# A gated mix of attention and a token MLP on one core: zeros, key sets, query transfers and value buffers scheduled anew

## The chip, the cores and the metric

The kernel runs on one core of a Trainium2 chip. The time is the device time of one execution in microseconds (us), the median of several runs. The core has these engines, each with its own instruction list that it works through in order: TensorE (PE; its weight loads are PEld), VectorE (DVE), ScalarE (ACT), GpSimd (POOL) and SyncE (SP, which here issues transfers and passes semaphores on). Transfers run on 16 DMA engines that the issuing engine's queue feeds.

## What is computed

The input x has 2048 tokens of 448 numbers. A gate weighs two branches, multi-head attention with 16 heads of 28 and a token-wise MLP of width 1792:

```python
x = A_x
g = _sigmoid((x * gate_w).sum(-1, keepdims=True))
a = _A_ref(x, A_wqkv, A_wo)      # softmax(q k^T * 28**-0.5) v, heads joined, @ wo
b = _B_ref(x, B_w1, B_b1, B_w2, B_b2)   # gelu(layernorm(x) @ w1 + b1) @ w2 + b2
return g * a + (1 - g) * b
```

All in fp32. Products on PE take fp32 in a rounded form (fp32r), so the kernel splits operands into a high part and a low part (value minus high) and sums three products; hence names like `hh`/`hl`, `ka`/`la`, `yh`/`yl`.

## The kernel before

**Three stages.** The first (0 to about 129 us) projects x to queries and keys (`QK`, stored to the DRAM tensor `qk`) and to values (`Val`, stored to `vs`). The second (to about 447 us) is the MLP in four chunks of 512 tokens: `Up` (x @ w1, one piece for each of 14 blocks of 128 of the width, then GELU on ACT) and `Down` (@ w2, one piece for each of four token tiles). The third is attention: scores, exponentials, products with the values, then the output projection.

**Four strips.** In the first two stages nearly every matmul contracts over 32 rows, a quarter of PE's array, and four of them run beside each other, one in each *strip* of 32 rows. A piece is done strip by strip; when a strip has finished its share, a semaphore passed through SP (`hand`, line 512) lets the next strip continue in the same PSUM bank. The class `Strips` plans all of this in Python while the kernel is built: it keeps a clock for each strip and engine from a table of costs, and lets each strip take the next matmul that its clock allows. Its result is a fixed instruction list for each engine. Tasks with a due time (`st.at(time, fn)`) are put into the lists when the planner's clock passes that time; `st.get(t, kb)` is its estimate of when a transfer of kb KB is in place: it queues all transfers noted so far at 230 KB per us and adds 2.2 us.

**Row maxima.** Softmax needs the maximum of each score row. The class `RowMax` computes plain scores (line 199, keys `kd` and queries `qd`, 28 rows of one strip) and DVE reduces them from PSUM (line 201). There are 16 sets (four groups of four heads, four chunks of queries) of 64 products, 1024 in all. Strip j holds head j of the group. After the 16th product of a set in a strip, the planner schedules three kinds of task: a query load two sets ahead (`load_q`, line 185), at the end of a group a load of the next group's keys (`load_k`, line 179), both on SP, and the closing of the set. These products are slipped between the pieces; what is left of them when attention begins is done there. `self.hot[j]` is the planner's time from which strip j may use its keys.

**Low parts.** The closing of an `Up` piece is: ACT writes GELU to `h` (line 342, two buffers), ACT writes the high part `hh[f]` (line 343), POOL writes the low part `hl[f]` (line 350). `Down` reads both.

**From the MLP to attention.** When the last `Up` piece of the last chunk is closed, `early` schedules the first group's attention operands: POOL sets the key low-part tile `la` to zero (line 829), loads queries (`fetch_qq`, line 802) and keys (`fetch_kk`, line 785) through its own queue, loads values from `vs` (`load_v`, line 797), and splits keys and queries into high and low parts (lines 790, 791, 806, 807).

**Attention.** The main loop works in turns. A turn does five or six score blocks (line 1121, three products each on one strip), two exponentials on ACT (line 1125; one over three blocks, one over two or three) and products with the values (line 1133):

```python
owed = rowmax.left()
size = min(left, 5 if owed and owed > 2 * ((left - 116) // 6) else 6)
```

While many row maxima are owed, a turn has five blocks and leaves room for three of them on the strips that its blocks do not use; with six blocks there is room for two. The last group's turns also hold output projections (`project`, lines 970 to 972).

**Values.** `Val.close` copies a value tile from PSUM to one of three buffers `vt` (line 311) and then issues its transfer to `vs` on ACT's queue (line 315). POOL writes the buffers' constant columns at the very start (lines 842 and 843).

Of the kernel before, what the change touches and what calls it, by code (L numbers as in the profile page):

```python
# [7 lines left out]
F32 = mybir.dt.float32  # L8
# [7 lines left out]
P = 128  # L16
S = 2048
D = 448
H = 16
# [16 lines left out]
def kernel(ctx: ExitStack, tc: tile.TileContext, xt, wqk, wv, wo, xk, w1, b1, w2, b2,  # L36
                          ident_d, sel_d, out):
    nc = tc.nc
# [35 lines left out]
    bk = banks.tile([P, 8, CH], F32, name="bk")  # L74
# [3 lines left out]
    px = p0.enter_context(tc.tile_pool(name="px", bufs=1))  # L78
# [42 lines left out]
    mr = px.tile([P, 2, NT], F32, name="mr")  # L121
    mrt = px.tile([P, 2 * NT], F32, name="mrt")
    std = px.tile([P, NT], F32, name="std")
    vt = [px.tile([P, H, 32], F32, name=f"vt{i}") for i in range(3)]

    bxr = [px.tile([P, 2, D], F32, name=f"bxr{i}") for i in range(2)]

# [96 lines left out]
    rowmax = RowMax()  # L224
# [63 lines left out]
    class Val(Piece):  # L288
# [18 lines left out]
            return ops  # L307

        def close(self, st, now):
            v, ps, tt = vt[self.i % 3], bk[:, self.bank], self.i  # L310
            nc.scalar.activation(v[:, :, 0:DH], ps[:, :D].rearrange("p (h d) -> p h d", d=DH), AF.Copy)
            nc.scalar.activation(zall[:, tt:tt + 1], ps[:, D:D + 1], AF.Copy)
            st.use("act", now + 0.2, 0.75)
            st.free[self.bank] = st.act + 0.1
            st.at(st.act + 0.3, lambda: nc.scalar.dma_start(vs[tt], v.rearrange("p (g j) d -> p g (j d)", g=NG)), act=0.35)
# [75 lines left out]
    class Strips:  # L391
# [92 lines left out]
        def rowmax(self, s, now):  # L484
            if now < self.hot[s] or not rowmax.ready(s):
                return False
            if rowmax.cnt[s] > 5 + min(rowmax.cnt):
                return False
            b = min(self.rm, key=lambda b: self.rm[b])
            if self.rm[b] > now:  # L490
                return False
            ends = rowmax.one(s, bk[:, b])
            self.t[s] = now + 0.232
            self.use("dve", now + 0.45, RM)
            self.rm[b] = self.dve + 0.1
            for kind, n, j in ends:
                if kind == "q":
                    self.at(now + 1.5, lambda n=n, j=j: rowmax.load_q(n, j))
                elif kind == "k":
                    self.at(now + 1.5, lambda n=n, j=j: rowmax.load_k(n, j))  # L500
                    self.hot[j] = now + 8.0
                else:
                    self.at(now + 0.5, lambda n=n: rowmax.close(n), dve=0.45)
                    self.at(now + 3.0, lambda n=n: rowmax.store(n))
            return True
# [277 lines left out]
    def fetch_kk(g, j):  # L783
        r = D + (4 * g + j) * DH
        loads[0].dma_start(klo[g][32 * j:32 * j + DH].bitcast(F32), qk[r:r + DH])

    def split_kk(g, i):
        sl = slice(i * CH, (i + 1) * CH)
        h, l = khi[g][:, sl], klo[g][:, sl]
        nc.gpsimd.tensor_copy(h, l.bitcast(F32))  # L790
        nc.gpsimd.tensor_sub(l, l.bitcast(F32), h.bitcast(F32))
# [27 lines left out]
    def early(st, now):  # L819
# [5 lines left out]
        ka, kb, la, lb = (ak.tile([P, S], F32R, name=n) for n in ("ka", "kb", "la", "lb"))  # L825
        va, vb = (ak.tile([P, NT, P], F32, name=n) for n in ("va", "vb"))
        for d, a, b in ((khi, ka, kb), (klo, la, lb), (vg, va, vb)):
            d.update({0: a, 1: b, 2: a, 3: b})
        st.at(now + 0.5, lambda: nc.gpsimd.memset(la.bitcast(F32), 0.0), pool=2.2)
        for j in range(4):  # L830
            st.at(now + 3.5 + 1.5 * j, lambda j=j: fetch_qq(0, j))
            st.at(now + 4.0 + 1.5 * j, lambda j=j: fetch_kk(0, j))
            st.at(now + 13.0 + 2.0 * j, lambda j=j: split_kk(0, j), pool=1.9)
        st.at(now + 12.0, lambda: split_qq(0), pool=1.9)
        st.at(now + 10.0, lambda: load_v(0, slice(0, 8)))
        st.at(now + 11.5, lambda: load_v(0, slice(8, 16)))
# [19 lines left out]
    load = [("wq", 0)] + [("x", 0, t) for t in range(4)] + [("wq", 3), ("wq", 4)]  # L856
# [365 lines left out]
```

## Time and profile before

| | |
|---|---|
| median of 3 runs | 1092.6 us (1090.66 to 1093.17) |
| the profiled execution, its own time | 1092.28 us |
| its span, first to last instruction | 1090.3 us |
| mean TensorE clock granted | 0.999 |
| matmuls on PE | 13314 |
| row maxima on DVE | 1024 |
| exponentials on ACT (line 1125) | 395 |
| first score matmul (line 1121) | 448.61 us |
| last exponential begins | 1066.93 us |

A profile row of the timeline reads: start in us, length in us, engine and line, operation, output <- inputs, shapes, count, and in brackets how long the engine had been idle and what ended that. A row of the waits reads: who waited, for whom, us in total, how many times, the longest. A row of windows reads: stretch, length, then for each engine its busy time with the number of its instructions, the granted clock, the busy share of the DMA engines and GB/s. A releaser is the one that came last by the profile; where that one had long been done, it was another.

### The profile page before, as it was taken

The page shows a single profiled execution, that of the slowest core. Times are in us where ns is not written, and L with a number is a line of the kernel's source. Part 1 is how long each engine was busy: PE and PEld are TensorE (multiplying, and loading weights), DVE is VectorE, ACT ScalarE, POOL GpSimd, SP SyncE. Part 2 cuts the span into 40 slices and gives each one's busy share as a digit, 9 for nine tenths or more (in the row PEclk, how much of TensorE's full clock was granted, in tenths as well). Part 3 has the DMA queues.
Part 4 walks back from the last instruction along what each step waited for, and adds up shares of the span by engine and source line. Part 5 has one row for each costly group of instructions (what it writes and reads, how often), then busy time and mean ns, then how long its engine had stood idle before and what let it go on. Part 6 is the DMA issues. An engine that isn't in the chain of part 4 may idle for free.

```text
span 1090.3 us, 30784 instructions
## 1 busy us (share of the span) xinstructions
PE 1075.4 (99%) x13314; PEld 728.4 (67%) x13314; DVE 740.5 (68%) x1186; ACT 636.0 (58%) x668; POOL 364.1 (33%) x372
## 2 busy tenths in 40 slices
PE   9999999999999999999999999999999999999997
PEld 6999999999999999644444444444444444454555
DVE  4279998999999998667766766567667766421102
ACT  5324472142141151577878878878877888858571
POOL 3456687345242057321100110310011215345430
PEclk9999999999999999999999999999999999999999
DMA  6695433104100105410000000500002101011111
GB/s 231 207 307 191 168 119 113 43 5 103 38 9 11 38 9 127 115 44 27 16 17 19 23 23 17 125 17 12 23 18 61 50 16 54 25 52 38 61 53 60
DMA packets 47463, 73.17 MB, mean 67 GB/s; under 512 B 13632, under 2 KB 28608, under 8 KB 46416
## 3 DMA queue, kind: packets, MB, share of 16 engines
q1 hardware_dynamic: 33888, 39.11, 12.2%
q0 software_dynamic: 4800, 16.89, 5.4%
q10 hardware_dynamic: 8640, 15.21, 3.8%
q8 instruction: 104, 1.70, 0.6%
q14 instruction: 31, 0.25, 0.1%
HBM read 51.75 MB, written 19.31 MB: 65 GB/s over the span
## 4 chain that ended last, share of the span: by engine, by line
PE 95%; DVE 2%; ACT 1%; DMA 0%; issue 0%; POOL 0%; SPq 0%; ACTq 0%; DVEq 0%; POOLq 0%
PE bk L475 33%; PE bk L1133 22%; PE bk L1121 19%; PE bk L199 15%; PE bk L970 1%; DVE mx L201 1%; PE bk L971 1%; PE bk L972 1%; PE bk L886 1%; ACT p L1125 1%; DMA first<-in_xt 0%; DVE ob L992 0%; POOL hl L350 0%; DVE acc L977 0%; ACT h L342 0%
## 5 line engine op out<-in xcount | busy, mean ns | idle before, releaser
L201 DVE TENSOR_REDUCE mx<-bk 128x1 f32<-128x512 f32 x1024 | 672.2, 688 | 197.7 <-PE bk L199 159.0
L1125 ACT ACTIVATE p<-bk 128x1536 f32<-128x1536 f32 (+1 forms) x395 | 483.1, 1275 | 135.7 <-PE bk L1121 134.9
L199 PE MATMUL bk<-kd,qd 28*128 28x512 f32 x1024 | 447.4, 438 | 3.1 <-DVE mx L201 1.9
L199 PEld LDWEIGHTS bk<-kd,qd 28*128 28x128 f32 x1024 | 186.1, 182 | 197.2 <-DVE mx L201 133.9
L475 PE MATMUL bk<-yh,w1f 32*128 32x512 f32 x1568 | 183.3, 392 | 0.4 <-ACT gb L385 0.4
L475 PE MATMUL bk<-yl,w1f 32*128 32x512 f32 x784 | 160.8, 391 | 0.0
L475 PEld LDWEIGHTS bk<-yh,w1f 32*128 32x128 f32 x1568 | 151.4, 183 | 2.2 <-ACT gb L385 1.6
L475 PE MATMUL bk<-w2h,hh 32*128 32x448 f32 x896 | 133.3, 366 | 1.3 <-ACT hh L343 1.3
L475 PE MATMUL bk<-w2l,hh 32*128 32x448 f32 x896 | 132.6, 363 | 0.0
L1133 PE MATMUL bk<-p,va 128*32 128x512 f32 x1024 | 131.2, 602 | 0.0
L1133 PE MATMUL bk<-p,vb 128*32 128x512 f32 (+1 forms) x1168 | 129.6, 548 | 0.0
L350 POOL TENSOR_TENSOR hl<-h,hh 128x512 fp32r<-128x512 f32 x56 | 73.7, 1325 | 132.4 <-ACT hh L343 67.1
L806 POOL CAST yh<-yl 128x512 fp32r<-128x512 f32 x16 | 9.8, 613 | 294.1 <-DMA yl<-qk 121.7
L1121 PE MATMUL bk<-yh,ka 29*128 29x512 f32 x512 | 106.9, 482 | 0.3 <-ACT h L385 0.3
L475 PEld LDWEIGHTS bk<-yl,w1f 32*128 32x128 f32 x784 | 103.7, 183 | 0.2
L475 PEld LDWEIGHTS bk<-w2h,hh 32*128 32x128 f32 x896 | 99.0, 183 | 1.9 <-ACT hh L343 1.7
L475 PEld LDWEIGHTS bk<-w2l,hh 32*128 32x128 f32 x896 | 100.0, 183 | 0.2
L1121 PE MATMUL bk<-yh,kb 29*128 29x512 f32 x512 | 99.1, 479 | 0.8 <-ACT p L1125 0.6
L1121 PE MATMUL bk<-yh,la 28*128 28x512 f32 x512 | 88.4, 392 | 0.0
L385 ACT ACTIVATE gb<-bk 128x448 f32<-128x448 f32 x14 | 7.6, 546 | 138.5 <-PE bk L475 100.2
L475 PE MATMUL bk<-w2h,hl 32*128 32x448 f32 x896 | 87.7, 362 | 0.0
L1121 PE MATMUL bk<-yl,ka 28*128 28x512 f32 x512 | 87.1, 410 | 0.0
(141 smaller groups left out, 1598.1 us busy)
## 6 DMA issues: line engine op xcount, KB each, us to landing
qk<-qo ACTq DMA_DIRECT2D x28, 256.0 KB
raw<-in_xt SPq DMA_DIRECT2D x17, 256.0 KB
vs<-vt ACTq DMA_DIRECT2D x16, 256.0 KB
rc<-rls SPq DMA_DIRECT2D x60, 64.0 KB
bxr<-in_xk POOLq DMA_DIRECT2D x8, 448.0 KB, 6.2
acc<-gbs SPq DMA_DIRECT2D x16, 224.0 KB
out_y<-acc SPq DMA_DIRECT2D x16, 224.0 KB
qd<-qk SPq DMA_DIRECT2D x60, 56.0 KB
```

The source lines that it names most:

```text
L199: nc.tensor.matmul(ps, self.qd[n % 2][r, i * P:(i + 1) * P], self.kd[r, k * 512:(k + 1) * 512], start=True, stop=True)
L201: nc.vector.reduce_max(self.mx[n % 2][:, j, i, k:k + 1], ps, axis=AX)
L350: nc.gpsimd.tensor_sub(hl[f], h, hh[f].bitcast(F32))
L475: mm = nc.tensor.matmul(bk[:, x.bank, :n], a, b, start=x.first, stop=(len(x.rem) == 1 and m == len(ops) - 1), skip_group_check=True)
L806: nc.gpsimd.tensor_copy(h, l.bitcast(F32))
L886: nc.tensor.matmul(bk[:, b], w, v, start=(i == 0), stop=(i == len(ops) - 1), skip_group_check=True)
L970: nc.tensor.matmul(po, h, woh[:, g], start=(g == 0), stop=False, skip_group_check=True)
L971: nc.tensor.matmul(po, h, wol[:, g], start=False, stop=False, skip_group_check=True)
L972: nc.tensor.matmul(po, l, woh[:, g], start=False, stop=(g == NG - 1), skip_group_check=True)
L1121: nc.tensor.matmul(bk[:, turn_bank(i)], w[r, ks], q[r], start=(p == 0), stop=(p == 2), skip_group_check=True)
L1125: nc.scalar.activation(t[:, :count], bk[:, b:b + count], AF.Exp, scale=SCALE)
L1133: nc.tensor.matmul(bk[32 * j:32 * j + 32, 7, sl], vg[n // NC][:, k, 32 * j:32 * j + 32], prob[4 * b + j][:, sl], start=(k == 0), stop=(k = ...
```

## The change

Four edits. In `early` the zeros for `la` get a later due time, the key loads, and with them the key splits, too. In `Strips.rowmax` the query load is due 6.0 instead of 1.5 after the strip's last product of a set; and a strip's new keys may be used from the planner's own estimate of their landing plus 1.0, taken at the moment when the load is issued (until then never), instead of a fixed 8.0 after the last product. The key loads are now also noted in the planner's transfer queue. The value buffers become five.

```diff
-    vt = [px.tile([P, H, 32], F32, name=f"vt{i}") for i in range(3)]
+    vt = [px.tile([P, H, 32], F32, name=f"vt{i}") for i in range(5)]
...
-            v, ps, tt = vt[self.i % 3], bk[:, self.bank], self.i
+            v, ps, tt = vt[self.i % 5], bk[:, self.bank], self.i
...
                 if kind == "q":
-                    self.at(now + 1.5, lambda n=n, j=j: rowmax.load_q(n, j))
+                    self.at(now + 6.0, lambda n=n, j=j: rowmax.load_q(n, j))
                 elif kind == "k":
-                    self.at(now + 1.5, lambda n=n, j=j: rowmax.load_k(n, j))
-                    self.hot[j] = now + 8.0
+                    def load(n=n, j=j):
+                        rowmax.load_k(n, j)
+                        self.hot[j] = self.get(self.clock + 0.6, 224) + 1.0
+
+                    self.at(now + 1.5, load)
+                    self.hot[j] = 1e9
...
-        st.at(now + 0.5, lambda: nc.gpsimd.memset(la.bitcast(F32), 0.0), pool=2.2)
+        st.at(now + 4.0, lambda: nc.gpsimd.memset(la.bitcast(F32), 0.0), pool=2.2)
         for j in range(4):
             st.at(now + 3.5 + 1.5 * j, lambda j=j: fetch_qq(0, j))
-            st.at(now + 4.0 + 1.5 * j, lambda j=j: fetch_kk(0, j))
-            st.at(now + 13.0 + 2.0 * j, lambda j=j: split_kk(0, j), pool=1.9)
+            st.at(now + 6.5 + 1.5 * j, lambda j=j: fetch_kk(0, j))
+            st.at(now + 14.5 + 2.0 * j, lambda j=j: split_kk(0, j), pool=1.9)
```

Four lines are added, so a line behind the change has a number higher by four in the changed kernel (829 becomes 833). Because the planner draws the order from these times, the lists of PE, SP and DVE differ from the first change of key sets on. Three places follow; the numbers behind tile names only tell buffers apart.

POOL at the end of the last `Up` pieces, where `la` is set to zero, before:

```order
L350 TENSOR_TENSOR hl_2820<-h,hh_2806 128x512
L350 TENSOR_TENSOR hl_2821<-h,hh_2807 128x512
L829 MEMSET la 128x2048
L350 TENSOR_TENSOR hl_2822<-h,hh_2808 128x512
L350 TENSOR_TENSOR hl_2823<-h,hh_2809 128x512
L350 TENSOR_TENSOR hl_2824<-h,hh_2810 128x512
L802 DMA yl<-qk 28x512
L785 DMA la<-qk 28x2048
```

and with the change:

```order
L350 TENSOR_TENSOR hl_2826<-h,hh_2812 128x512
L350 TENSOR_TENSOR hl_2828<-h,hh_2814 128x512
L350 TENSOR_TENSOR hl_2827<-h,hh_2813 128x512
L350 TENSOR_TENSOR hl_2829<-h,hh_2815 128x512
L350 TENSOR_TENSOR hl_2830<-h,hh_2816 128x512
L806 DMA yl<-qk 28x512
L833 MEMSET la 128x2048
L806 DMA yl<-qk 28x512
L789 DMA la<-qk 28x2048
```

The zeros stood ahead of three low parts and stand behind all of them now, and ahead of three of the four query loads.

SP at the first change of key sets (`kd` keys, `qd` queries, `ms` maxima of a closed set, `raw` the next chunk's x), before:

```order
L220 DMA ms_74<-mt_156 4x32x32
L185 DMA qd_151<-qk 28x512
L179 DMA kd<-qk 28x2048
L185 DMA qd_151<-qk 28x512
L179 DMA kd<-qk 28x2048
L185 DMA qd_151<-qk 28x512
L179 DMA kd<-qk 28x2048
L185 DMA qd_151<-qk 28x512
L179 DMA kd<-qk 28x2048
L552 DMA raw_132<-in_xt 128x512
```

and with the change:

```order
L220 DMA ms_74<-mt_158 4x32x32
L185 DMA qd_152<-qk 28x512
L179 DMA kd<-qk 28x2048 x2
L185 DMA qd_153<-qk 28x512
L179 DMA kd<-qk 28x2048 x2
L556 DMA raw_132<-in_xt 128x512
```

A query load stood ahead of each of the four key loads; one is left between them, and the other three follow behind the loads of x.

ACT where the turns of five blocks end (128x1536 is an exponential over three blocks, 128x1024 over two), before:

```order
L1125 ACTIVATE p_14640<-bk 128x1536
L1125 ACTIVATE p_14652<-bk 128x1024
L1125 ACTIVATE p_14671<-bk 128x1536
L1125 ACTIVATE p_14683<-bk 128x1024
L1125 ACTIVATE p_14711<-bk 128x1536
L1125 ACTIVATE p_14723<-bk 128x1024
L1125 ACTIVATE p_14744<-bk 128x1536
L1125 ACTIVATE p_14756<-bk 128x1024
```

and with the change:

```order
L1129 ACTIVATE p_14662<-bk 128x1536
L1129 ACTIVATE p_14675<-bk 128x1536
L1129 ACTIVATE p_14694<-bk 128x1536
L1129 ACTIVATE p_14706<-bk 128x1024
L1129 ACTIVATE p_14734<-bk 128x1536
L1129 ACTIVATE p_14747<-bk 128x1536
L1129 ACTIVATE p_14768<-bk 128x1536
L1129 ACTIVATE p_14780<-bk 128x1024
```

Turns of six appear earlier. In the whole list the exponentials over two blocks go from 161 to 158 and those over three from 234 to 236; the last turn has five blocks instead of three. The list of PE has 537 products of line 199 ahead of the first score matmul, where it had 529.

## The prediction

> **What bounds the kernel now.** I read the page first, then which waits TensorE (PE) ends on, then the places of those waits in time. The page:
>
> ```profile
> span 1090.3 us, 30784 instructions
> PE 1075.4 (99%) x13314; PEld 728.4 (67%) x13314; DVE 740.5 (68%) x1186; ACT 636.0 (58%) x668; POOL 364.1 (33%) x372
> ...
> L201 DVE TENSOR_REDUCE mx<-bk 128x1 f32<-128x512 f32 x1024 | 672.2, 688 | 197.7 <-PE bk L199 159.0
> ```
>
> PE is busy for 99% of the span, so the other engines matter only where they make it stop or make its list longer. What stops it from the key-set change to the scores, by the waits of PE between 240 and 450 us:
>
> ```profile
> engine line waited for: us in total, times, longest us
> PE bk L475 <- ACT hh L343: 1.3, 1, 1.3
> PE bk L199 <- DVE mx L201: 1.0, 1, 1.0
> PE bk L1121 <- ACT h L385: 0.3, 1, 0.3
> ```
>
> Two stops, 2.3 us together, and the change has an edit for each. The first, in the timelines of POOL, ACT and PE:
>
> ```profile
> 404.59 1.30 POOL L350 TENSOR_TENSOR hl<-h,hh 128x512 fp32r<-128x512 f32 x1 [0.28 <-POOL hl L350]
> 405.83 1.81 POOL L829 MEMSET la<- 128x2048 f32 x1
> 407.59 2.52 POOL L350 TENSOR_TENSOR hl<-h,hh 128x512 fp32r<-128x512 f32 x2
> ...
> 405.93 0.69 ACT L342 ACTIVATE h<-bk,b1s 128x512 f32<-128x512 f32 x1 [0.22 <-POOL hl L350]
> 408.93 0.69 ACT L342 ACTIVATE h<-bk,b1s 128x512 f32<-128x512 f32 x1 [1.65 <-POOL hl L350]
> 409.65 0.63 ACT L343 ACTIVATE hh<-h 128x512 fp32r<-128x512 f32 x1
> ...
> 408.48 0.52 PE L475 MATMUL bk<-w2l,hh 32*128 32x448 f32 x4
> 410.33 0.48 PE L475 MATMUL bk<-w2h,hh 32*128 32x448 f32 x4 [1.33 <-ACT hh L343]
> ```
>
> The zeros for la sit among the last low parts hl. h has two buffers, so ACT's last GELU waits until POOL has read an older h; POOL spends 1.81 us on zeros first. Hence the hole of 1.33 us on PE ahead of 410.33. The second stop, from the timelines of SP, PE and DVE, a window, and the transfers of 255 to 268 us:
>
> ```profile
> 257.80 0.38 SPq L179 DMA_DIRECT2D kd<-qk  x1
> 258.71 1.24 SPq L179 DMA_DIRECT2D kd<-qk  x1
> ...
> 265.23 0.47 PE L199 MATMUL bk<-kd,qd 28*128 28x512 f32 x1 [0.95 <-DVE mx L201]
> ...
> 265.74 4.63 DVE L201 TENSOR_REDUCE mx<-bk 128x1 f32<-128x512 f32 x7 [1.23 <-PE bk L199]
> ...
> 264.00:266.00 2.00, 1.05 (x22) 0.77 (x20) 0.77 (x2) 0.00 (x0) 0.00 (x0) 1.00 0.99 231
> ...
> lnr<-lns POOLq DMA_DIRECT2D x1, 512.0 KB, 6.9
> ```
>
> PE is busy 1.05 of 2 us: 0.95 us lost, ahead of a product on kd. DVE is named as releaser, but it had been done, and itself waited 1.23 us for PE (the L201 row of the page gives 688 ns for one of its maxima). What is late is the third strip's key rows, issued at 257.80 and in use at 265.23, which is 7.4 us, with the DMA engines 99% busy at the end of it and a 512 KB load of lnr (6.9 us) in the same stretch.
>
> **The change part by part.** *Zeros.* They move behind the last hl, so the chain is 1.8 us shorter at that place. PE gains the hole, 1.33 us, and the thinning ahead of it (four matmuls start at 408.48, none after them): I take 1.5, bounds 1.2 and 1.8. Three query loads, four key loads and the splits on POOL now stand behind the zeros and later by up to 3 us. Cover: the splits of set 0 end at 430, POOL then waits, and the first score matmul is at 448.61:
>
> ```profile
> 428.79 1.29 POOL L791 TENSOR_TENSOR la<-la,ka 128x512 fp32r<-128x512 f32 x1
> 445.96 0.56 POOL L941 CAST woh<-ob 128x448 fp32r<-128x448 f32 x1 [13.13 <-PE bk L199]
> 448.61 0.50 PE L1121 MATMUL bk<-yh,ka 29*128 29x512 f32 x3 [0.28 <-ACT h L385]
> ```
>
> 13 us of room for 3; without it the delay would fall on PE whole. Price 0.
>
> *Key sets.* The old rule let a strip use its new keys 8.0 us after its last maximum of the old set. The new one waits for the load to be issued (1.5 us), then adds 0.6, 224/230 and 2.2 for the transfer, plus 1.0: 4.8 us from the issue, 6.3 in all, and more only when the planner has noted other transfers in the queue. So on an empty queue the set is used 1.7 us *earlier* than before. Against that the key loads now go out ahead of the query loads, which stood before each of them in SP's queue; the row at 257.80 would be about one issue (1.0 us) earlier, and closer to being ahead of lnr's 512 KB. Bounds: the whole 0.95 gained, or a wait of 7.4 − 4.8 = 2.6 us in place of it, a loss of 1.65. I take a gain of 0.7, since only one strip of the four made PE wait, and by an eighth of its 7.4 us. The second set of keys does not stop PE now (issued from 429.06, first product 435.61, so at most 6.5 us):
>
> ```profile
> 429.06 0.38 SPq L179 DMA_DIRECT2D kd<-qk  x1
> 435.61 0.49 PE L199 MATMUL bk<-kd,qd 28*128 28x512 f32 x1
> ```
>
> "DMA: Bandwidth & Descriptors" of the Trainium skill, section "Anatomy of one DMA — SWDGE (gpsimd) path", fits a transfer as a fixed 2.0 us plus its bytes at 436 GB/s; our estimate from it for 224 KB is 2.5 us. The row shows 7.4, so the measurement decides here. By the page 4.8 us is ample at both key sets, the wait is gone whole, and the sum below is 0.25 us lower; no run here shows such a load with the DMA engines idle.
>
> *Query transfers* go out 6.0 us after the strip's last maximum, not 1.5. They feed the set after the next, 64 maxima of 688 ns on DVE away, 44 us. PE's list of waits has none for qd; SP waits for PE ahead of some of them (its waits, 240 to 300 us):
>
> ```profile
> SPq L185 <- PE bk L199: 7.8, 3, 7.0
> ```
>
> A later issue has less of that to wait. Price 0, bounds −0.2 and +0.2 (the hand-off signals between strips are in the same queue).
>
> *Five value buffers.* Two more pairs of memsets at the very start, and ACT's copies into vt, by the waits of ACT and the timeline of POOL:
>
> ```profile
> ACT vt L311 <- PE bk L475: 22.3, 15, 4.2
> 1.00 0.14 POOL L843 MEMSET vt<- 128x48 f32 x1
> 4.07 1.01 POOL L96 TENSOR_TENSOR wq<-first,wq 128x384 fp32r<-128x384 f32 x1 [2.92 <-ACT wq L92]
> ```
>
> All waits of the copies end on PE, none on the transfer out of vt, so three were enough. Four memsets at under 0.14 us vanish in 2.92 idle. Price 0.
>
> *The list of PE itself.* The planner's order changes from the first key change on: 537 row maxima stand ahead of the first score matmul, where there were 529. The stage's pace and a thin place in it:
>
> ```profile
> 17.00:446.90 429.90, 426.27 (x7293) 408.87 (x7291) 376.79 (x605) 139.97 (x248) 211.99 (x215) 1.00 0.32 100
> 300.00:318.00 18.00, 18.00 (x315) 17.65 (x312) 17.70 (x30) 7.83 (x12) 7.73 (x6) 1.00 0.05 13
> 318.00:326.00 8.00, 8.00 (x117) 7.53 (x117) 7.81 (x13) 5.17 (x8) 3.96 (x4) 1.00 0.01 2
> ```
>
> 429.9 us for 7293 matmuls is 59 ns each; eight more cost 0.5. PE counts as busy in the third row too, yet it starts 117 matmuls in 8 us where the second row's pace gives 140: 23 at 57 ns, 1.3 us, lost because a piece waits for another and its strip stands still. An order drawn anew can have one such place more or fewer: bounds −1.3 and +1.3. I take +0.7, half of one more, because maxima placed earlier push products of the pieces back, and the four strips must all end before the scores begin.
>
> *The scores.* Eight maxima fewer are left for them, and their turns get cheaper: 161 turns of five score blocks, 36 of six and one of three become 157, 39 and a last one of five. Exponentials by window, two to a turn:
>
> ```profile
> 450.00:920.00 470.00, 378.04 (x320) 1.00 0.14 37
> 927.40:958.90 31.50, 27.78 (x20) 1.00 0.07 22
> ```
>
> A turn of five takes 470/160 = 2.94 us, one of six 31.5/10 = 3.15. −4 × 2.94 + 3 × 3.15 = −2.3, and two blocks more in the last turn, a third of 3.15, give +1.05: −1.25. By the maxima alone (2.94 less five sixths of 3.15 is 0.31 for three, so 0.10 each) it is −0.85. I take −1.0.
>
> Sum: −1.5 − 0.7 + 0.5 + 0.7 − 1.0 = −2.0 us. The profiled execution took 1092.28 us, its span and 2.0 around it, giving 1090.3; it lies 0.3 below the median of 1092.6, whose runs reach from 1090.66 to 1093.17. From the median it would be 1090.6; I say 1090.4.
>
> **The rivals.** *Both waits vanish, and the new order is no thinner:* −1.8 − 0.95 + 0.5 + 0 − 1.25 = −3.5, about 1089.0. For it: the key loads overtake the query loads, and the Trainium skill's transfer law above. Against: the 7.4 us.
>
> *The gain is spent in the new order:* a whole thin place more, and the key wait stays: −1.5 + 0 + 0.5 + 1.3 − 1.0 = −0.7, 1091.8. For it: 117 against 140, a loss that no wait row names. Against: the stage has several such places already, and the number of them need not grow.
>
> *Slower: the keys are used too soon.* If a load takes 7.4 us at the first set again and 6.5 at the second, a rule of 4.8 makes PE wait 2.6 and 1.7 us where it waited 0.95 and 0; PE takes its matmuls in order, so every strip stands behind the one that waits, and DVE behind them. −1.5 + 1.65 + 1.7 + 0.5 + 0.7 − 1.0 = +2.1, about 1094.6. It decides from landings later than 4.8 us after the issue on. Against: 6.5 is a bound, not a landing, and the planner adds its noted queue, lnr's 512 KB among it when that is issued first.
>
> **How the numbers follow.** The forecast gets 0.45, both waits gone 0.24, gain spent 0.18, slower 0.13. About 0.2%, 2.2 us, is what a measurement of this kernel can tell from no change; from 1092.6 that is 1090.4, the middle of the forecast. So half of the forecast and the second case are faster, 0.47; the other half and the third case are the same, 0.40; the last is slower, 0.13. The range reaches from 1088.3 (below the second case by the uncertainty of the maxima) to 1092.9, past the third, and leaves most of the slower case out. The forecast's own range is 1089.2 to 1091.6.
>
> **What would show it.** The waits of PE should have no stop on hh near 409 and POOL's zeros behind the last hl; wrong if the last GELU still waits over 1 us for POOL. At the first key change the window that held 1.05 of 2 us should be nearly full; a longer wait of L199, or one near the second set, makes the slower rival right. The first score matmul should stand about 1 us earlier than 448.61 and the last exponential some 2 us earlier; if the first comes no earlier although both stops are gone, the new order spent them. A wait of ACT on the transfers out of vt, now or then, would make the buffers' zero wrong.

## The result, and the profile after

| | before | changed |
|---|---|---|
| first comparison, median of 6 runs each | 1093.14 us | 1088.28 us |
| ratio, 95% interval | | 0.9959, 0.9946 to 0.9972 |
| the changed kernel again, 8 runs beside 19 of before | 1092.22 us | 1088.42 us |
| ratio, 95% interval | | 0.9966, 0.9951 to 0.9981 |
| span of the profiled execution | 1090.3 us | 1086.6 us |

The change makes the kernel faster by 3.7 to 4.5 us (0.34% to 0.41%, the two ratios times 1092); the forecast was 2.0 us. The six runs of before in the first comparison were on the high side (1093.14, where 35 and 26 later ones have medians of 1091.94 and 1091.31), so the lower figure is the better one. It may still be high: of the runs in the second comparison of the table 7 of the 19 of before and 3 of the 8 of the changed kernel had a mean granted clock of 0.998 or lower, and the medians of the others, 1091.01 and 1088.18 us, are 2.8 us apart. The spans of the two profiles differ by 1090.3 − 1086.6 = 3.7 us as well, but 1.0 of it is an earlier start that belongs to the execution (see the control).

The page after. TensorE's work is the same to 0.1 us, so what went, the 1.0 us at the start included, is time in which it stood still:

```profile
span 1086.6 us, 30783 instructions
PE 1075.5 (99%) x13314; PEld 729.7 (67%) x13314; DVE 738.9 (68%) x1186; ACT 635.2 (58%) x667; POOL 363.4 (33%) x376
```

Windows of before at four places (start:end, length, then busy time and number of instructions of PE, PEld, DVE, ACT, POOL, then the granted clock, the busy share of the DMA engines and GB/s):

```profile
206.00:211.00 5.00, 4.58 (x79) 4.13 (x76) 4.37 (x7) 1.55 (x3) 0.00 (x0) 1.00 0.42 147
255.00:262.00 7.00, 7.00 (x126) 6.85 (x126) 5.88 (x12) 0.00 (x0) 2.29 (x3) 1.00 0.64 135
262.00:270.00 8.00, 7.05 (x132) 6.67 (x129) 6.74 (x11) 0.00 (x0) 2.62 (x3) 1.00 0.71 193
404.00:412.00 8.00, 6.67 (x123) 6.11 (x121) 6.30 (x11) 5.81 (x9) 7.14 (x7) 1.00 0.01 4
```

The same windows of the changed kernel:

```profile
206.00:211.00 5.00, 5.00 (x88) 4.67 (x81) 4.84 (x9) 1.50 (x3) 0.00 (x0) 1.00 0.42 153
255.00:262.00 7.00, 7.00 (x138) 6.83 (x133) 6.76 (x13) 0.00 (x0) 0.80 (x2) 1.00 0.86 201
262.00:270.00 8.00, 8.00 (x154) 7.87 (x150) 7.98 (x13) 0.00 (x0) 5.86 (x5) 1.00 0.42 143
404.00:412.00 8.00, 8.00 (x154) 7.38 (x152) 7.71 (x15) 4.85 (x8) 7.56 (x8) 1.00 0.05 11
```

Read the first number behind the length, and the count behind it. Three places stopped TensorE before and are full now: 0.42 us at 209, 0.95 us at 265, 1.33 us at 409. The first of them is not in the prediction, whose list of waits began at 240 us.

At 409, the timeline of POOL in the changed kernel has the zeros (L833, which was L829) behind the last hl:

```profile
404.91 2.60 POOL L350 TENSOR_TENSOR hl<-h,hh 128x512 fp32r<-128x512 f32 x2 [0.21 <-PE bk L199]
407.73 1.29 POOL L350 TENSOR_TENSOR hl<-h,hh 128x512 fp32r<-128x512 f32 x1 [0.22 <-PE bk L199]
...
409.52 1.83 POOL L833 MEMSET la<- 128x2048 f32 x1
```

and in ACT's the last GELU waits 0.15 us for POOL, where it waited 1.65:

```profile
406.24 0.69 ACT L342 ACTIVATE h<-bk,b1s 128x512 f32<-128x512 f32 x1 [0.15 <-POOL hl L350]
```

At the keys, SP's timeline in the changed kernel has the third and fourth key load at 255.19, ahead of three query loads, where they were issued at 257.80 and 258.71 (1.0 us of the difference is the earlier start). They still stand 0.14 us behind POOL's load of lnr, which goes out at 255.05:

```profile
254.49 0.37 SPq L185 DMA_DIRECT2D qd<-qk  x1
255.19 0.73 SPq L179 DMA_DIRECT2D kd<-qk  x2
256.03 3.14 SPq L556 DMA_DIRECT2D raw<-in_xt  x4
...
259.86 3.02 SPq L185 DMA_DIRECT2D qd<-qk  x3
```

The turn from the strips to the scores was not in the sum either. Before, from the first work of the attention on PE to the first exponential on ACT is 449.99 − 447.13 = 2.86 us:

```profile
447.13 1.19 PE L914 MATMUL bk<-ka 128*128 128x512 f32 x4
...
449.63 0.50 PE L1121 MATMUL bk<-yh,ka 29*128 29x512 f32 x2
...
449.99 2.37 ACT L1125 ACTIVATE p<-bk 128x1536 f32<-128x1536 f32 x2 [0.42 <-PE bk L1121]
```

and in the changed kernel it is 446.66 − 444.52 = 2.14 us. The first score matmul no longer waits for ACT's copy (0.28 us before), and the rest of the first blocks follows at once, 0.60 us behind it in place of 449.63 − 448.61 = 1.02:

```profile
444.52 1.19 PE L918 MATMUL bk<-ka 128*128 128x512 f32 x4
445.64 0.50 PE L1125 MATMUL bk<-yh,ka 29*128 29x512 f32 x3
...
446.24 0.59 PE L1125 MATMUL bk<-yh,ka 29*128 29x512 f32 x2
...
446.66 2.37 ACT L1129 ACTIVATE p<-bk 128x1536 f32<-128x1536 f32 x2 [0.47 <-PE bk L1125]
```

### The profile page after: what moved, and what is told of

Same layout as the page of the kernel before. It is cut to its first block, busy times and chain, and to the rows that moved or that the text cites. A ratio compares the mean times of both kernels' runs of the same rounds, so it can differ in the third digit from the quotient of the medians.

```text
span 1086.6 us, 30783 instructions
## 1 busy us (share of the span) xinstructions
PE 1075.5 (99%) x13314; PEld 729.7 (67%) x13314; DVE 738.9 (68%) x1186; ACT 635.2 (58%) x667; POOL 363.4 (33%) x376
## 4 chain that ended last, share of the span: by engine, by line
PE 96%; DVE 1%; ACT 1%; DMA 0%; issue 0%; DVEq 0%; SPq 0%; ACTq 0%
PE bk L475 34%; PE bk L1137 22%; PE bk L1125 19%; PE bk L199 15%; PE bk L974 1%; PE bk L975 1%; PE bk L976 1%; PE bk L890 1%; ACT p L1129 1%; DVE mx L201 1%; DMA first<-in_xt 0%; DVE ob L996 0%; PE bk L918 0%; DMA gbs<-gb 0%; DVE acc L981 0%
## 5 line engine op out<-in xcount | busy, mean ns | idle before, releaser
L475 PE MATMUL bk<-yh,w1f 32*128 32x512 f32 x1568 | 186.4, 392 | 0.1
L475 PE MATMUL bk<-yl,w1f 32*128 32x512 f32 x784 | 164.7, 391 | 0.0
L475 PE MATMUL bk<-w2h,hl 32*128 32x448 f32 x896 | 90.2, 362 | 0.0
```

What stands on the lines that cost most here:

```text
L475: mm = nc.tensor.matmul(bk[:, x.bank, :n], a, b, start=x.first, stop=(len(x.rem) == 1 and m == len(ops) - 1), skip_group_check=True)
```

## The experiments

Two durations are compared below beside the times. "Strips" runs from the first strip matmul on TensorE to the first exponential, "scores" from there to the end of the span; both are read from the timelines of one profiled execution. The first strip matmul itself began anywhere from 15.90 to 18.35 us, without regard to the kernel, so the span alone says less than these.

| kernel | median, us | ratio to before, 95% | strips, us | scores, us |
|---|---|---|---|---|
| before | | | 432.67 | 640.30 |
| before, as a control | 1092.48 | 1.0002, 0.9991 to 1.0014 | 433.40 | 640.37 |
| value buffers alone | 1093.07 | 1.0007, 0.9995 to 1.0019 | 432.37 | 641.57 |
| queries alone | 1090.07 | 0.9983, 0.9971 to 0.9996 | 430.73 | 639.97 |
| zeros alone, list of before | 1090.61 | 0.9990, 0.9977 to 1.0004 | 431.42 | 640.48 |
| zeros alone, planner told | 1089.78 | 0.9990, 0.9980 to 1.0000 | 430.14 | 640.53 |
| rule for keys alone | 1094.41 | 1.0029, 1.0019 to 1.0038 | 435.68 | 639.55 |
| changed, queries early | 1091.65 | 1.0002, 0.9993 to 1.0012 | 433.46 | 638.42 |
| changed, old rule for keys | 1088.29 | 0.9968, 0.9956 to 0.9980 | 429.41 | 640.59 |
| changed | 1088.28 | 0.9959, 0.9946 to 0.9972 | 430.33 | 639.92 |
| changed, again | 1088.42 | 0.9966, 0.9951 to 0.9981 | 429.97 | 639.68 |
| before, lnr behind the keys | 1090.48 | 0.9986, 0.9974 to 0.9998 | 431.21 | 640.24 |
| changed, old rule, lnr behind the keys | 1087.78 | 0.9956, 0.9939 to 0.9973 | 428.56 | 640.31 |
| the same, keys after 10.0 us | 1087.12 | 0.9951, 0.9933 to 0.9969 | 427.71 | 640.79 |

### The control

No edit.

> The kernel before, unchanged, run as if it were an experiment: the ratio should be 1.000 within 0.002. It also tells how much the start moves by itself: the first strip matmul began at 17.32 us in the profile of before and at 16.33 in that of the changed kernel, with the same instructions ahead of it. If the 1.0 us is a matter of the run, this profile may show either; the stops of TensorE at 208.96 to 209.56 (1.9 us), at 265 (2.6 us with those of its neighbours) and at 409 to 410 (1.7 us) should all be there again.

Measured 1.0002 (0.9991 to 1.0014), and all three stops are there again; the one at the keys is larger in this execution, 1.41 us of 8 in place of 0.95:

```profile
206.00:211.00 5.00, 4.51 (x77) 4.12 (x77) 4.30 (x7) 1.63 (x3) 0.00 (x0) 1.00 0.42 152
262.00:270.00 8.00, 6.59 (x122) 6.19 (x118) 6.27 (x11) 0.00 (x0) 2.47 (x2) 1.00 0.67 169
```

The expectation gives larger sizes for the stops (1.9, 2.6 and 1.7 us); no view here shows them, and what is compared below is the time missing in these windows. The first strip matmul is at 16.63 us, 0.7 earlier than in the first profile of the same kernel. So the 1.0 us by which the changed kernel's profile began earlier belongs to the execution, not to the change.

### Queries alone

```diff
-                    self.at(now + 1.5, lambda n=n, j=j: rowmax.load_q(n, j))
+                    self.at(now + 6.0, lambda n=n, j=j: rowmax.load_q(n, j))
```

> The kernel before with the query transfers 6.0 us behind the end of their strip in place of 1.5, and nothing else; TensorE's list is that of before. First theory (order in SP's queue): the third and fourth key loads were late because SP handed query loads out ahead of them and stood in them; with those later the keys are issued near 255 in place of 257.8, the stop near 265 (1.3 us net) goes without any new rule for keys, and so does the one at 209 (0.45 us net): about 1.8 us less, ratio 0.998 to 0.9985. Rival (landing): the keys land late because another queue's packets are ahead of theirs, and the stop went in the changed kernel because its list uses the keys later: the stop at 265 stays here, at most 0.45 us is gained, ratio 0.9995 to 1.000. What the prediction said (query transfers worth 0 within 0.2 us) is the rival's number or better.

Measured 0.9983 (0.9971 to 0.9996), about 1.9 us less, from the edit to which the prediction gave nothing. Two stops are gone, and the third is untouched:

```profile
206.00:211.00 5.00, 5.00 (x86) 4.57 (x82) 4.84 (x9) 1.09 (x2) 0.00 (x0) 1.00 0.46 166
262.00:270.00 8.00, 8.00 (x153) 7.97 (x151) 7.89 (x13) 0.00 (x0) 6.36 (x6) 1.00 0.33 116
404.00:412.00 8.00, 6.69 (x123) 6.18 (x118) 6.23 (x13) 2.82 (x4) 7.70 (x12) 1.00 0.25 61
```

So it went as the first theory said; by the rival the stop at 265 would have stayed. What stood behind the query load at 209 is in SP's own waits, 198 to 214 us of the kernel before:

```profile
SPq L185 <- PE bk L475: 6.4, 1, 6.4
```

A query load came up before its tile was free (its wait ends on TensorE) and held SP's queue for 6.4 us; behind it stood the signals (L512) that hand a tile from strip to strip. With the load later SP has no such row in that stretch. That these signals made the stop at 209 is read from the order of SP's list; no run moved them alone.

### Zeros alone

The planner keeps its account of the zeros at the old time, so that TensorE's list does not move:

```diff
-        st.at(now + 0.5, lambda: nc.gpsimd.memset(la.bitcast(F32), 0.0), pool=2.2)
+        st.at(now + 0.5, lambda: None, pool=2.2)
+        st.at(now + 4.0, lambda: nc.gpsimd.memset(la.bitcast(F32), 0.0))
...
-            st.at(now + 4.0 + 1.5 * j, lambda j=j: fetch_kk(0, j))
-            st.at(now + 13.0 + 2.0 * j, lambda j=j: split_kk(0, j), pool=1.9)
+            st.at(now + 6.5 + 1.5 * j, lambda j=j: fetch_kk(0, j))
+            st.at(now + 14.5 + 2.0 * j, lambda j=j: split_kk(0, j), pool=1.9)
```

> The kernel before with the zeros for the keys 3.5 us later, and the key loads and splits behind them later as in the change, while the planner's account keeps the zeros at their old time, so that TensorE's list is that of before. Theory: the stop of TensorE near 408.5 to 410.3 (1.66 us) is gone, what follows is earlier by as much, and the end with it: 1.5 to 1.7 us less, ratio 0.9985. Rival: the gain is taken back at the turn from strips to scores, where the first score matmuls wait for something that does not move: the stop goes, the first score is earlier by under 0.5 us, ratio 1.000.

Measured 0.9990 (0.9977 to 1.0004): about 1.1 us less by the ratio, and the interval does not quite leave 1. The profile is plainer than the time. The hole at 409 is filled, and this execution lost at the keys instead, 1.92 us of 8:

```profile
262.00:270.00 8.00, 6.08 (x112) 5.68 (x109) 5.69 (x9) 0.00 (x0) 3.45 (x3) 1.00 0.59 141
404.00:412.00 8.00, 8.00 (x155) 7.59 (x151) 7.80 (x16) 4.95 (x8) 7.74 (x8) 1.00 0.04 11
```

The rival, that the turn to the scores takes the gain back, is not seen: the first score matmul is at 446.27 us, 2.3 earlier, and the scores take 640.48 us, as before. The same edit with the planner told, which draws the list anew ("the kernel just above" in its expectation is the changed kernel with the old rule for keys, shown further down):

> The kernel before with the later zeros, key loads and splits alone, and the planner told of them; the list of TensorE is that of the kernel just above from the zeros on, with the planner's end at 421.8 us against 422.4 of before. Theory: the stop at 409 to 410 is gone (1.66 us) and 0.6 us of modelled gain may come with it; the stops at 209 and 265 stay: 1.7 to 2.3 us less, ratio 0.998 to 0.9985. Rival: the moved splits and loads of keys come too late for the first scores and give 1 us or more back there: ratio 0.999 to 1.000.

Measured 0.9990 (0.9980 to 1.0000), about 1.1 us less. That is the rival's number, but its reason is not seen: the profile has scores of 640.53 us, as before, and strips of 430.14 us, 2.7 less than the mean of the three profiles with the list and the stops of before (432.8). Three of its 11 runs had a mean granted clock of 0.998 or lower and a median of 1092.30, the other eight 1089.68; the last section shows one thing that lowers the clock.

### Value buffers alone

```diff
-    vt = [px.tile([P, H, 32], F32, name=f"vt{i}") for i in range(3)]
+    vt = [px.tile([P, H, 32], F32, name=f"vt{i}") for i in range(5)]
...
-            v, ps, tt = vt[self.i % 3], bk[:, self.bank], self.i
+            v, ps, tt = vt[self.i % 5], bk[:, self.bank], self.i
```

> The kernel before with five buffers for the values in place of three, and nothing else. Theory: nothing waits for the third buffer, so no change, ratio 1.000 within 0.001, and TensorE's three places of stops as before. Rival: ScalarE's evictions waited there for the stores of the values and held banks; then the stops at 209 would shrink by up to 0.45 us here.

Measured 1.0007 (0.9995 to 1.0019): nothing that can be told from none. The stop at 209 is as it was, so it does not come from the values:

```profile
206.00:211.00 5.00, 4.54 (x78) 3.97 (x75) 4.34 (x8) 1.63 (x4) 0.00 (x0) 1.00 0.43 152
```

### The rule for keys alone

```diff
-                    self.at(now + 1.5, lambda n=n, j=j: rowmax.load_k(n, j))
-                    self.hot[j] = now + 8.0
+                    def load(n=n, j=j):
+                        rowmax.load_k(n, j)
+                        self.hot[j] = self.get(self.clock + 0.6, 224) + 1.0
+
+                    self.at(now + 1.5, load)
+                    self.hot[j] = 1e9
```

> The kernel before with the new rule for keys alone: a key set is used from its modelled landing and not from 8.0 us behind the end of its strip; TensorE's list is word for word that of the changed kernel, query transfers, zeros and buffers are as before. The planner's own end of the strips is 1.7 us later than before. First theory (the rule itself lifts the stop): no stop near 265, that at 409 to 410 stays, the redrawn list costs about 0.5 us net: about 1.3 less for the stop, 0.5 more for the list, ratio 0.999 to 1.000. Second theory (the query transfers lift the stop): it stays in part, 0.5 us or more of it, ratio 1.000 to 1.001. Third (the redrawn list itself gains, at the turn from strips to scores and in them): 1.2 us less there and no loss ahead of it, ratio 0.997 to 0.998.

All three expectations were too low: measured 1.0029 (1.0019 to 1.0038), 3.2 us slower than before. By itself the rule is the slower rival of the prediction. The planner uses the keys sooner, the query loads still stand between the key loads in SP's queue, and TensorE stands 2.11 us ahead of a product on kd (the profile names no releaser):

```profile
263.95 0.46 PE L199 MATMUL bk<-kd,qd 28*128 28x512 f32 x1 [2.11 <-issue]
```

The windows around it show a second cost:

```profile
260.00:262.00 2.00, 1.84 (x35) 1.45 (x27) 1.96 (x3) 0.00 (x0) 0.00 (x0) 1.00 1.01 216
262.00:264.00 2.00, 0.05 (x4) 0.08 (x4) 0.00 (x0) 0.00 (x0) 0.00 (x0) 1.00 0.99 216
264.00:266.00 2.00, 2.00 (x28) 1.96 (x32) 1.29 (x2) 0.00 (x0) 0.00 (x0) 0.64 0.97 195
266.00:268.00 2.00, 2.00 (x28) 2.00 (x24) 1.15 (x3) 0.00 (x0) 0.00 (x0) 0.51 0.96 306
268.00:270.00 2.00, 2.00 (x43) 2.00 (x42) 1.80 (x4) 0.00 (x0) 1.88 (x2) 1.00 0.24 73
```

For four microseconds behind the stop the granted clock is 0.64 and 0.51, and TensorE starts 28 matmuls in 2 us where it starts 43 after: 30 matmuls lost, at 2/43 us each 1.4 us more. PE counts as 2.00 of 2.00 busy there; only the clock column and the counts tell.

One row of this run bears on another edit. Its zeros have their old due time, and yet TensorE does not stop between 404 and 412 us, where it was busy for 6.67 of 8 us before:

```profile
404.00:412.00 8.00, 8.00 (x130) 7.61 (x127) 7.84 (x13) 5.10 (x9) 3.90 (x4) 1.00 0.01 2
```

In the redrawn list the zeros, at 411.87 us, stand ahead of the last two low parts and no longer of three, and the last GELU, at 411.97, does not wait for them.

### The changed kernel with early queries

```diff
-                    self.at(now + 6.0, lambda n=n, j=j: rowmax.load_q(n, j))
+                    self.at(now + 1.5, lambda n=n, j=j: rowmax.load_q(n, j))
```

> The changed kernel with the query transfers back at 1.5 us; TensorE's list is that of the changed kernel. If the query transfers lift the stop of the keys, it is back here with 0.5 to 1.3 us, and that at 209 with 0.45: time 1.0 to 1.8 us above the changed kernel, ratio to before 0.997. If the rule for keys lifts it, only the 0.45 us at 209 come back: ratio 0.996 to 0.9965. If query transfers are worth nothing, the ratio is that of the changed kernel, 0.996.

Measured 1.0002 (0.9993 to 1.0012): one number taken back, and the whole gain of the change is gone, which is more than any of the three expected. TensorE's list is that of the changed kernel. Its timeline names the transfer, whose landing ends the wait 9.36 us behind the last key load's issue at 257.59:

```profile
266.95 0.46 PE L199 MATMUL bk<-kd,qd 28*128 28x512 f32 x1 [1.36 <-DMA kd<-qk]
```

Both stops are back, with that at 409 still filled:

```profile
206.00:211.00 5.00, 4.61 (x78) 4.04 (x76) 4.41 (x8) 1.70 (x4) 0.00 (x0) 1.00 0.43 152
...
262.00:270.00 8.00, 6.64 (x119) 6.17 (x117) 6.23 (x10) 0.00 (x0) 2.66 (x3) 1.00 0.71 169
404.00:412.00 8.00, 8.00 (x143) 7.55 (x139) 7.70 (x13) 7.20 (x11) 6.78 (x6) 1.00 0.02 4
```

The two stops are 0.39 and 1.36 us, and the strips are 3.3 us longer than the mean of the changed kernel's two profiles (430.15). Part of the rest is thinning that does not count as a stop: from 262 to 270 us 119 matmuls start where the changed kernel starts 154. Seven of the 11 runs have a mean granted clock of 0.998 or lower, with a median of 1092.61 against 1091.07 of the other four. What else is lost stays open.

### The changed kernel with the old rule for keys

```diff
-                    def load(n=n, j=j):
-                        rowmax.load_k(n, j)
-                        self.hot[j] = self.get(self.clock + 0.6, 224) + 1.0
-
-                    self.at(now + 1.5, load)
-                    self.hot[j] = 1e9
+                    self.at(now + 1.5, lambda n=n, j=j: rowmax.load_k(n, j))
+                    self.hot[j] = now + 8.0
```

> The changed kernel with the old rule for keys (8.0 us behind the end of their strip) and all else as changed; the planner puts the end of the strips at 421.8 us in place of 424.2. If the query transfers alone lift the stop of the keys, nothing stands near 265, the strips end up to 2.4 us sooner than in the changed kernel, and the time is below it: ratio 0.994 to 0.9955. If the rule is needed, a stop of 1 us or more stands near 265 and the ratio is 0.996 or above. If the redrawn list of the changed kernel is what gains (turn to the scores, scores), that gain is missing here: ratio 0.997 or above.

Measured 0.9968 (0.9956 to 0.9980), beside 0.9966 of the changed kernel run again: with late queries the new rule for keys is worth nothing that can be told in the time. The signs are those of the second expectation, though: a stop of 1.21 us near 265 and a ratio above 0.996. So late queries alone do not always lift the stop; the kernel with late queries and nothing else, which has the same rule, had none. SP's rows differ: the last two key loads, at 256.82, stand 0.12 us behind POOL's load of lnr, as they do there (0.10) and in the changed kernel (0.14), but here issuing the two took 1.67 us in place of 0.74, so that the fourth came later. Why it took longer, no run shows:

```profile
256.82 1.67 SPq L179 DMA_DIRECT2D kd<-qk  x2
...
262.00:270.00 8.00, 6.79 (x126) 6.43 (x123) 6.50 (x11) 0.00 (x0) 2.54 (x3) 1.00 0.73 195
```

Its strips are shorter all the same (429.41 us), because the planner's list ends 2.4 us sooner by its own account (421.8 and 424.2). That gains about what the stop costs.

### lnr behind the keys

```diff
-        nc.gpsimd.dma_start(lnr[c], lns.rearrange("(n t) i -> n (t i)", n=2)[:, cs].partition_broadcast(P))
+        (nc.sync if c == 3 else nc.gpsimd).dma_start(lnr[c], lns.rearrange("(n t) i -> n (t i)", n=2)[:, cs].partition_broadcast(P))
```

> The kernel before with the fourth load of lnr (512 KB, at 256.55 us) taken from POOL's queue and put behind the keys in SP's, ahead of the four loads of raw; TensorE's list, zeros, queries and buffers are as before. First theory (landing): the keys land late because lnr's packets run beside them; then the stop in the window from 262 to 270 us (0.95 us of 8 in before, 1.41 in the control) is gone, although the query loads still stand ahead of the keys, and 1.0 to 1.4 us are gained, ratio 0.9985 to 0.999. Second theory (order): the query loads ahead of the keys in SP's queue make them late; the stop stays, ratio 1.000. The stop at 209 stays by both.

Measured 0.9986 (0.9974 to 0.9998), 1.5 us less; beside the 12 of its 19 runs of before with a clock above 0.998 (1091.01) the median is only 0.5 us lower, so the profile is the firmer evidence. The query loads still stand between the keys, and the stop is gone:

```profile
255.97 0.31 SPq L185 DMA_DIRECT2D qd<-qk  x1
256.33 0.38 SPq L179 DMA_DIRECT2D kd<-qk  x1
256.83 0.31 SPq L185 DMA_DIRECT2D qd<-qk  x1
257.24 0.32 SPq L179 DMA_DIRECT2D kd<-qk  x1
257.73 0.40 SPq L160 DMA_DIRECT2D lnr<-lns  x1
```

```profile
206.00:211.00 5.00, 4.51 (x77) 4.09 (x72) 4.33 (x8) 1.63 (x3) 0.00 (x0) 1.00 0.42 152
...
262.00:270.00 8.00, 8.00 (x155) 7.92 (x153) 7.90 (x13) 0.00 (x0) 4.15 (x4) 1.00 0.49 155
```

So the keys were late because 512 KB of another queue ran beside them. The packet times of the traces say the same. In before, lnr's packets moved from 258.0 to 262.9 us, and those of the fourth key load, issued at 258.71, only from 262.9 to 265.7; here that load, issued at 257.24, moved from 258.9 to 260.9. That it went out a little sooner is not the reason: in the changed kernel with early queries it was issued as soon after the first key load (7.11 us, here 7.15), and with lnr beside it its packets ended 7.8 us behind its issue, here 3.7.

The order in SP's queue matters in so far as it lets the keys out before lnr's packets start, which is 1.5 to 1.9 us behind lnr's own issue. This is how late queries help although the last keys are issued behind lnr: there the fourth key load went out 1.2 us ahead of lnr's first packet, in the changed kernel 1.3, and neither stopped; in the changed kernel with the old rule it went out just as lnr's packets began, and TensorE stopped. The stop at 209 is untouched, as both theories had it.

### The changed kernel again, and two kernels made from what was found

> The changed kernel once more, beside other kernels and far more runs of the one before. Its first comparison had six runs of before with a median of 1093.14 us, where 35 and 26 later runs had 1091.94 and 1091.31. Theory: part of its 4.5 us was that sample; the true gain is near 3.5 us, ratio 0.9965 to 0.997, that is no better than the changed kernel with the old rule for keys (0.9968), so the new rule for keys is worth nothing once the query transfers are late. Rival: the rule is worth 1 us or more, ratio 0.996 or below again. The windows from 206 to 211 and from 262 to 270 us should be full.

Measured 0.9966 (0.9951 to 0.9981), as the theory had it. Both windows are full again.

The old rule for keys with lnr behind the keys:

> The changed kernel with the old rule for keys, and the fourth load of lnr put behind the keys in SP's queue. The kernel without this last edit still stopped for 1.2 us in the window from 262 to 270 us, with its ratio at 0.9968. If lnr's packets are what the keys wait for, that stop is gone and the ratio is 0.9955 to 0.996, about 1 us below the changed kernel. If not, the stop is there and the ratio is that of the kernel without the edit.

Measured 0.9956 (0.9939 to 0.9973), and the stop that the same list had without the edit is gone:

```profile
262.00:270.00 8.00, 8.00 (x148) 7.60 (x147) 7.62 (x12) 0.00 (x0) 4.87 (x4) 1.00 0.47 151
```

Its median is 0.6 us below that of the changed kernel in the same comparison (1087.78 and 1088.42), less than was expected and well inside the intervals.

The last kernel adds

```diff
-                    self.hot[j] = now + 8.0
+                    self.hot[j] = now + 10.0
```

> The kernel just above with a new key set used from 10.0 us behind the end of its strip in place of 8.0; the planner's own end of the strips is 421.4 us in place of 421.8 (424.2 in the changed kernel). With 2 us more for the keys no stop is expected in the window from 262 to 270 us whatever lnr does. If the planner's end is what the chip shows, the ratio is 0.995 to 0.9955, the fastest of all; if the strips only stand idle elsewhere for the later keys (fewer matmuls begun in a window that counts as full), 0.9965 or above.

Measured 0.9951 (0.9933 to 0.9969), with the shortest strips of all, 427.71 us:

```profile
262.00:270.00 8.00, 8.00 (x152) 7.84 (x148) 7.99 (x14) 0.00 (x0) 5.19 (x5) 1.00 0.53 154
```

Its median is 1.3 us below that of the changed kernel in the same comparison (1087.12 and 1088.42). The intervals of the two ratios overlap widely, so that it beats the changed kernel is likely, not shown.

## Why the prediction was right, and where its sum was not

The direction was right. The size, −3.7 to −4.5 us, lies beyond the forecast (−2.0) and a little beyond the rival in which both waits vanish (−3.5), and the first median, 1088.28 us, is at the very edge of the range (1088.3). That it came out so near is partly luck: the largest single gain came from an edit priced at nothing, and the cost of the new order was priced too high. Nor do the edits add up one by one: alone they bring −1.9 (queries), −1.1 (zeros), nothing (buffers) and +3.2 (the rule for keys), which makes +0.2, and together −3.7.

Means over the profiles stand for the pieces: strips 432.8 us in the three with the list and the stops of before, 430.15 in the two of the changed kernel, so −2.65; scores 640.75 and 639.8, so −0.95. Together −3.6, beside −3.7 by the second ratio. The first score matmul, forecast to stand about 1 us earlier, is at 445.64 in place of 448.61; 1.0 of these 3.0 us is the earlier start.

- *Zeros, −1.5 (1.2 to 1.8).* The mechanism is right for the list of before: the hole of 1.33 us is filled where the zeros moved and stays where they did not, and the thinning ahead of it is seen in the counts: 123 matmuls in 8 us before, 154 now, 31 at the stage's 59 ns, which is 1.8. In time the edit alone brings 1.1 us, with intervals that reach from 2.5 us to none. In the redrawn list the hole is gone even with the old due time, as the run with the rule for keys alone shows; what moving the zeros adds within the changed kernel, no run shows. The 13 us of cover for the later loads and splits of keys held.
- *Key sets, −0.7 (−0.95 to +1.65).* The wait went whole, about 1.0 by the mean of the three profiles (0.95, 1.41, 0.71). The rule for keys, the edit that was to lift it, does not do so by itself: alone it costs 3.2 us, and on top of late queries it is worth nothing that can be told in the time. Whether it helps there against the stop is open: with late queries the old rule stopped in one of two profiles and the new one in neither of two. The reason given second, that the keys go out ahead of the query loads and come closer to being ahead of lnr, is what the runs showed, and it belongs to the next edit.
- *Queries, 0 (±0.2).* This is the step that failed. Alone they bring 1.9 us, and without them the changed kernel gains nothing. The prediction looked for a wait on qd, and there was none; what the query loads delayed was what stood behind them in SP's queue, the key loads and the signals between strips. The signals were named as the reason for the ±0.2; the stop put down to them is 0.42 to 0.49 us. It lay at 209 us, outside the list of waits that was read.
- *Value buffers, 0.* Nothing seen (1.0007, 0.9995 to 1.0019).
- *Eight more maxima and the new order, +0.5 + 0.7.* Too high. The three stops are 0.45 + 1.0 + 1.6 = 3.05 us (the last taken between the hole of 1.33 and the count's 1.8), the strips gained 2.65, so by subtraction the list costs 0.4. This is loose: from the kernel with early queries, which has the same list, the same subtraction gives (433.46 − 0.39 − 1.36) − (432.8 − 3.05) = 2.0. Part of it is a turn to the scores that is 0.7 us shorter, a place for which the sum had no term. The thin place at 318 to 326, the reason for the +0.7, has only moved: 138 matmuls start there against 117, but 299 against 315 in the 18 us ahead of it.
- *Scores, −1.0.* The size fits, −0.95, but it is not measured that finely: the three profiles of the first mean reach from 640.30 to 641.57, and without the highest the difference is −0.5. That the last exponential would start 2 us earlier was too little: it ends at 1061.80 + 2.37 = 1064.2 in place of 1066.93 + 1.45 = 1068.4, 4.2 us earlier. Of this 1.0 is the earlier start, and there is one turn fewer (157 + 39 + 1 in place of 161 + 36 + 1).
- *The slower rival, +2.1.* Its mechanism is real at the first set of keys, and needs a condition that the change itself removes. With the query loads early, the rule of 4.8 us behind the issue is too short: 2.11 and 1.36 us of wait in the two kernels that have it. At the second set of keys neither stopped: their lists of TensorE's waits are empty from 270 to 470 us.

The Trainium skill's law of "DMA: Bandwidth & Descriptors" ("Anatomy of one DMA — SWDGE (gpsimd) path") gives an estimate of about 2.5 us for a key load; that page of the Trainium skill has the law for transfers issued by GpSimd. The key loads here are issued by SP. The sum by it came out 0.25 us nearer, but not by its reason: with the query loads early a key load landed 9.36 us or more behind its issue, with the DMA engines 0.91 to 1.04 busy from 260 to 266 us. The prediction says that no run shows such a load on idle engines. That is wrong, for the first key load of the same set is one. Before, SP issued a query load (56 KB) at 250.42 us and the key load (224 KB) at 250.84, and the windows around them are

```profile
250.00:251.00 1.00, 1.00 (x21) 0.98 (x22) 1.00 (x2) 1.00 (x3) 0.79 (x2) 1.00 0.00 0
251.00:252.00 1.00, 1.00 (x26) 1.00 (x23) 1.00 (x3) 1.00 (x3) 1.00 (x2) 1.00 0.42 107
252.00:253.00 1.00, 1.00 (x26) 1.00 (x24) 1.00 (x3) 0.34 (x1) 1.00 (x2) 1.00 0.49 180
253.00:254.00 1.00, 1.00 (x26) 1.00 (x22) 0.96 (x3) 0.00 (x0) 1.00 (x1) 1.00 0.01 0
```

The last two columns are the DMA engines' busy share and GB/s: 107 + 180 = 287 KB, which is both loads, have moved by about 253 us, 2.2 us behind the key load's issue. (The rows do not show when its semaphore followed.) The third key load, of the same size, took up to 7.4 us because of what ran beside it.

## What to carry to other kernels

Price an early transfer by what stands behind it in its queue, not by who needs its data: here moving loads that nobody waited for brought 1.9 us alone, and the two edits aimed at waits 1.1 us and a loss of 3.2. Read the list of waits over the whole stage, not only where the change is aimed. When a rule is made tighter and a neighbour is moved out of its way in the same change, try each without the other: the tight rule alone cost 3.2 us, and with the way clear it brought nothing that could be told.

## What the runs showed that was not expected

- A stop of 2.11 us on TensorE (the rule for keys alone) was followed by windows of 2 us at granted clocks of 0.64 and 0.51; a stop of 1.92 us at the same place in the kernel with the zeros alone left it at 1.00. The Trainium skill, "TensorE: Matmul & The Clock Gate", Part 1, gives idle time of about 3.4 us for the fall to half the clock, by a window that runs freely. That the low clock lasted (0.36 + 0.49) × 2 / 0.5 = 3.4 us at half speed fits that window; that 2.11 us of standing still sufficed does not fit its figure for the idle time.
- It may show in times, too: 8 of the 9 runs with the rule for keys alone had a mean clock of 0.998 or lower, 1 of the 26 runs of before beside them. But 7 of the 19 runs of before in the comparison with the changed kernel run again were as low, so the rule is not the only cause. In the profile the stop of 2.11 us cost 1.4 us more than itself.
- The same kernel's stop at the keys was 0.95 and 1.41 us in two executions (1.21 us in the changed kernel with the old rule, whose list is the same up to there but whose query loads are late): it is set by how the keys and lnr's load meet, and moving lnr alone made it vanish in both kernels in which that was tried.
- The start moves from run to run: the first strip matmul is at 15.90 to 18.35 us over 14 profiles, with the same loads ahead of it. That is two thirds of what this change is worth.
